# Hash attention, then a gated feed-forward block, on one core: hash bits made on four column quarters and sent by way of DRAM, a third buffer for the attention output, and another start

## The chip, the cores and the metric

The kernel runs on one core of one Trainium2 chip. The metric is the device time in microseconds, from start to end of one execution. The kernel before takes 933.71 us, the median of three executions (931.88 to 935.03).

A core has a matrix engine (TensorE, written PE in the views), a vector engine (VectorE, DVE), an activation engine (ScalarE, ACT), a general engine (GpSimd, POOL) and a queue engine (SyncE, SP). Each works through its own instructions in order, and they wait for each other by semaphores. Matrix products are written to PSUM, banks of accumulators that ScalarE and VectorE read. Transfers are issued by SyncE, ScalarE or GpSimd and run on 16 shared DMA engines.

## What is computed

Two stages. The first is attention for 4 batches x 8 heads, sequence 768, head size 64. Every query and key gets a bucket of six sign bits; a score counts only where the buckets of query and key are equal. The second is a feed-forward block over the 3072 tokens.

```python
q_bits = (np.einsum('bhsd,dk->bhsk', q, proj) > 0).astype(np.int64)   # proj: 64 x 6
k_bits = (np.einsum('bhsd,dk->bhsk', k, proj) > 0).astype(np.int64)
q_bucket = np.sum(q_bits * powers, axis=-1)
k_bucket = np.sum(k_bits * powers, axis=-1)
mask = q_bucket[:, :, :, None] == k_bucket[:, :, None, :]
scores = scale * np.matmul(q, k.transpose(0, 1, 3, 2))
scores = np.where(mask, scores, -1000000000.0)
scores = scores - np.max(scores, axis=-1, keepdims=True)
attn = np.exp(scores)
attn = attn / (np.sum(attn, axis=-1, keepdims=True) + 1e-09)
# (B,H,S,D) -> x: (B*S, H*D) = 3072 x 512
h = x @ w_in                                     # 512 x 2048
sp = np.maximum(h, 0.0) + np.log1p(np.exp(-np.abs(h)))
out = (h * erf(sp)) @ w_out                      # 2048 x 512
```

## The kernel before, where the change touches it

Heads are worked on in 16 pairs. A pair's q and k lie one head above the other, 64 partitions each. Names: `P` is 128 partitions, `S` = 768, `HS` = 384 (half a sequence), `D` = 64, `NBIT` = 6, `GC` = 3. A pair has four score groups n (two query halves, two key halves) of three score tiles c; `h` counts halves of pairs.

At the start, seven constant products in bfloat16 run on TensorE while the first loads come in:

```python
    nc.vector.memset(w_sum[:, 0, 0, 0:HS], 1.0)
    warm = w_sum[:, 0, 0, 0:HS].bitcast(BF16)
    proj_in = const.tile([P, 2 * NBIT], F32, name="proj_in")
    nc.scalar.dma_start(out=proj_in, in_=proj2)
# ... cut ...
            for n in range(WARM):                # WARM = 7
                nc.tensor.matmul(
                    out=bank("warm"),
                    lhsT=warm[:, 0:P],
                    rhs=warm[:, P : P + 512],
                    start=True,
                    stop=True,
                )
            for half in range(2):
                hash_bits(pairs[0], big, (half,))
                take_bits(pairs[0], bitp, (half,))
```

The hash bits: one float32 product per half and per q or k, each 64 output rows (32 for each head of the pair), in a PSUM tile called `bits`. ScalarE takes the sign into `qb`; VectorE writes the keys' signs, times a weight of 2**100 or 0, into `kb` for each head, and doubles the queries' signs:

```python
    def hash_bits(d, big, halves=(0, 1)):
        if halves[0] == 0:
            d["bits"] = big("bits")
        for half in halves:
            for n, what in enumerate("qk"):
                nc.tensor.matmul(
                    out=d["bits"][n * D : n * D + D, half, 0:HS],
                    lhsT=proj_sb,
                    rhs=d[what][:, half * HS : (half + 1) * HS],
                    start=True,
                    stop=True,
                )

    def sign_bits(d, bitp, cols):
        if cols.start == 0:
            for what in ("qb", "kb"):
                d[what] = bitp.tile([P, S], BF16, name=what, tag=what)
        nc.scalar.activation(
            out=d["qb"][:, cols].rearrange("p (h s) -> p h s", s=HS),
            in_=d["bits"][:, cols.start // HS : cols.stop // HS, 0:HS],
            func=AF.Sign,
            scale=2.0**100,
            bias=sgn[:, 0:1],
        )

    def spread_bits(d, cols, ab):
        nc.vector.tensor_scalar(
            out=d["kb"][ab * D : ab * D + D, cols],
            in0=d["qb"][D:P, cols],
            scalar1=weight[D:P, ab : ab + 1],
            scalar2=None,
            op0=ALU.mult,
        )

    def double_bits(d, cols):
        nc.vector.tensor_copy(out=d["qb"][D:P, cols], in_=d["qb"][0:D, cols])
```

A score tile is first the bfloat16 product of these masks (zero where the buckets agree, hugely negative elsewhere) and on top of it the float32 product of q and k:

```python
            def score(n, c):
                i, half, g = n // 4, n // 2 % 2, n % 2
                d = pairs[i]
                cols = slice(half * HS, (half + 1) * HS)
                keys = slice((g * GC + c) * P, (g * GC + c + 1) * P)
                st = d["st", n, c] = big("st")
                for part, src in enumerate(("b", "")):
                    for ab in range(2):
                        rows = slice(ab * D, ab * D + D)
                        nc.tensor.matmul(
                            out=st[:, ab, 0:HS],
                            lhsT=d["k" + src][rows, keys],
                            rhs=d["q" + src][rows, cols],
                            start=(part == 0),
                            stop=(part == 1),
                        )
```

The tiles `st` and `bits` share three slots in PSUM (`big`). ScalarE takes the exponential of a tile to SBUF (`exponential`), VectorE sums over the keys (`sum_keys`), TensorE multiplies by v (`weigh`, tile `av`) and spreads the sum (`divisor`, tile `z_ps`: four products of 32 output rows and 192 columns). ScalarE copies `av` to `x` (`leave`) and `z_ps` to `z`. The divisor goes to DRAM and back to lie on 128 partitions (`spread`, `gather`), is inverted, and comes back spread over the partitions as `r` (`widen`); `normalise` multiplies x by it and `send` stores x in `xs`. The buffers of x come from a ring of two, those of z and r together from another ring of two:

```python
            tc.tile_pool(name="xst", bufs=2) as xst,
# ... cut ...
            def home(i, what):
                if i < NPAIR - 1:
                    return xst.tile([P, S], F32, name=what, tag="x" if what == "x" else "z")
                rows = blocks[1][:, :, :].rearrange("p k t -> p (k t)")
                return rows[:, S : 2 * S] if what == "x" else rows[:, 0:S]

            def leave(h):
                i, half = divmod(h, 2)
                d = pairs[i]
                cols = slice(half * HS, (half + 1) * HS)
                if half == 0:
                    d["x"] = home(i, "x")
                nc.scalar.copy(out=d["x"][:, cols], in_=d["av"][:, 0:HS])
```

The products of TensorE stand in a fixed order, the other engines' instructions are put in order beforehand by a list scheduler in the kernel with estimated durations (`op(...)`). Bits of the next pair come at the first half of the pair before it:

```python
            chain = []
            order = [("score", 0)]
            for h in range(NH):
                order += [("score", n) for n in (2 * h + 1, 2 * h + 2) if n < NS]
                if h % 2 == 0 and h // 2 + 1 < NPAIR:
                    order.append(("bits", h // 2 + 1))
                if h >= 1:
                    order.append(("divisor", h - 1))
                order += [("weigh", 2 * h), ("weigh", 2 * h + 1)]
```

While attention runs, the weights of the second stage are fetched by GpSimd's queue in 30 pieces and converted from 64-bit words to float32 by ScalarE and VectorE.

## Time and profile before

| | before |
|---|---|
| median of three executions, us | 933.71 (931.88 to 935.03) |
| span of the profiled execution, us | 932.9 |
| TensorE busy, us | 916.8 (98%) |
| VectorE busy, us | 829.7 (89%) |
| ScalarE busy, us | 771.0 (83%) |
| GpSimd busy, us | 17.4 (2%) |
| moved by DMA | 80.92 MB, mean 87 GB/s |

The profile is of one execution. A row of a timeline reads: start in us from the start of the span, duration of the row in us, engine, line of the kernel, operation, tile written <- tiles read, shapes, how many instructions the row merges (x), and in brackets how long the engine stood idle before it and what ended that wait. A float32 product shows as two matmul records. The end of a matmul is modelled, so the distance of starts tells more than its duration. A row of the wait table reads: engine, tile and line that waited <- what ended the wait: us in total, times, longest us. Attention's lines are L358 (bits), L529 (scores), L635 (divisor), L602 (weighing), L543 (exponential), L659 (leave), L590 (sums over keys); the second stage's are L1098 and L1238.

### The profile page before, as it was taken

Reading aid. Unit: us, or ns where it says so; the run is one execution under the profiler, and the core shown is the slowest. Engines: PE = TensorE matmul, PEld = TensorE weight load, DVE = VectorE, ACT = ScalarE, POOL = GpSimd, SP = SyncE. Lnnn points to the kernel's source line nnn. Section 1 sums busy time; section 2 is a strip of 40 time slices with the busy share of each in tenths; the row PEclk is TensorE's granted clock in tenths of the full one; section 3 lists DMA queues with packets and bytes.
Section 4 is the critical chain, followed back from the end, with each engine's and each line's share of the span. In section 5 each row is a group of like instructions: output and inputs, shape, how many; then the busy total and the mean of one; then the engine's idle time right before and its main releaser. Section 6 shows DMA issues by size and latency. Waiting matters only on the chain.

```text
span 932.9 us, 12993 instructions
## 1 busy us (share of the span) xinstructions
PE 916.8 (98%) x5003; PEld 661.9 (71%) x5003; DVE 829.7 (89%) x1041; ACT 771.0 (83%) x1002; POOL 17.4 (2%) x35
## 2 busy tenths in 40 slices
PE   8999999999999999999999999999999999999996
PEld 3444444444444458888888888888888888888885
DVE  4999998999888997899999889998899789988995
ACT  5888787768876838999998998899989997899891
POOL 0000000000000000000000000000000000000000
PEclk9999999999999999999999999999999999999998
DMA  8365455576654322010212012210221111001211
GB/s 198 99 158 147 132 148 139 147 200 165 147 149 131 97 103 97 1 46 34 80 68 79 34 46 69 80 34 34 79 78 36 34 65 49 34 34 46 68 35 48
DMA packets 61398, 80.92 MB, mean 87 GB/s; under 512 B 33296, under 2 KB 46224, under 8 KB 61328
## 3 DMA queue, kind: packets, MB, share of 16 engines
q1 hardware_dynamic: 56672, 64.08, 23.9%
q0 software_dynamic: 4352, 15.73, 5.6%
q8 instruction: 41, 0.67, 0.3%
q10 hardware_dynamic: 304, 0.20, 0.1%
q14 instruction: 29, 0.24, 0.1%
HBM read 64.07 MB, written 15.93 MB: 86 GB/s over the span
## 4 chain that ended last, share of the span: by engine, by line
PE 85%; DVE 7%; DMA 4%; ACT 2%; issue 1%; SPq 0%; DVEq 0%; ACTq 0%
PE M L1238 30%; PE X L1098 27%; PE st L529 11%; PE av L602 9%; PE M L1098 3%; PE bits L358 2%; DMA xs<-x 1%; ACT e_all L543 1%; DVE x_sum L590 1%; PE z_ps L635 1%; DVE x L590 1%; DMA zd<-z 1%; DMA zc<-zd 1%; DVE x L721 1%; DMA r<-rd 1%
## 5 line engine op out<-in xcount | busy, mean ns | idle before, releaser
L1165 DVE SCALAR_TENSOR_TENSOR e<-w,e 128x1024 f32<-128x1024 f32 x144 | 173.4, 1221 | 5.8 <-ACT w L1161 3.0
L1161 ACT ACTIVATE w<-w,cq 128x1024 f32<-128x1024 f32 x144 | 160.7, 1143 | 1.9
L543 ACT ACTIVATE e_all<-st 128x768 f32<-128x768 f32 x192 | 149.1, 819 | 11.3 <-PE st L529 11.3
L529 PE MATMUL st<-q,k 64*128 64x384 f32 x768 | 156.6, 486 | 0.0
L1238 PE MATMUL M<-w_out_sb,h 128*128 128x256 f32 x576 | 140.2, 380 | 0.4 <-DVE h L1180 0.4
L602 PE MATMUL av<-e_all,v 128*64 128x385 f32 (+1 forms) x768 | 131.1, 490 | 0.0
L1098 PE MATMUL X<-x,w_in_sb 128*128 128x256 f32 x512 | 121.2, 380 | 0.0
L1238 PEld LDWEIGHTS M<-w_out_sb,h 128*128 128x128 f32 x576 | 109.3, 190 | 15.9 <-DVE h L1180 1.1
L1098 PEld LDWEIGHTS X<-x,w_in_sb 128*128 128x128 f32 x512 | 97.1, 190 | 13.8 <-ACT h L1116 0.6
L602 PEld LDWEIGHTS av<-e_all,v 128*64 128x64 f32 x768 | 52.4, 136 | 67.2 <-issue 65.4
L1238 PE MATMUL M<-wt,S 128*128 128x256 f32 x384 | 93.4, 379 | 0.4 <-DVE S L1195 0.4
L529 PEld LDWEIGHTS st<-q,k 64*128 64x128 f32 x768 | 69.1, 190 | 32.8 <-issue 32.1
L1098 PE MATMUL X<-x_sum,w_sum 128*128 128x256 f32 x344 | 81.7, 380 | 1.8 <-ACT h L1116 1.8
L1238 PEld LDWEIGHTS M<-wt,S 128*128 128x128 f32 x384 | 72.9, 190 | 10.7 <-DVE S L1195 0.8
L1098 PEld LDWEIGHTS X<-x_sum,w_sum 128*128 128x128 f32 x344 | 65.1, 190 | 12.0 <-ACT h L1116 3.3
L1116 ACT COPY h<-X 128x512 f32<-128x512 f32 x85 | 49.0, 577 | 22.3 <-PE X L1098 21.4
L1142 DVE SCALAR_TENSOR_TENSOR w<-w,e 128x1024 f32<-128x1024 f32 x48 | 58.4, 1221 | 9.6 <-ACT w L1137 9.3
L529 PE MATMUL st<-qb,kb 64*128 64x384 bf16 x384 | 63.7, 327 | 3.3 <-ACT e_all L543 3.2
L1180 DVE TENSOR_TENSOR h<-h,e 128x1024 f32<-128x1024 f32 x48 | 58.0, 1221 | 6.1 <-ACT e L1176 5.9
L659 ACT COPY x<-av 128x384 f32<-128x384 f32 x32 | 15.3, 478 | 57.4 <-DMA xs<-x 28.8
L1156 ACT ACTIVATE w<-e 128x1024 f32<-128x1024 f32 x48 | 50.4, 1050 | 13.3 <-DVE e L1152 13.0
L1152 DVE TENSOR_TENSOR e<-e,w 128x1024 f32<-128x1024 f32 x48 | 57.5, 1219 | 2.7 <-ACT e L1148 2.6
(117 smaller groups left out, 1421.0 us busy)
## 6 DMA issues: line engine op xcount, KB each, us to landing
wt<-wt SPq DMA_DIRECT2D x24, 768.0 KB, 4.3
raw<-in_w_out_dram POOLq DMA_DIRECT2D x16, 512.0 KB, 3.9
raw<-in_w_in_dram POOLq DMA_DIRECT2D x14, 512.0 KB, 4.2
v<-in_v_dram SPq DMA_DIRECT2D x32, 192.0 KB, 4.5
xs<-x SPq DMA_DIRECT2D x16, 384.0 KB, 2.4
q<-in_qkT_dram SPq DMA_DIRECT2D x30, 192.0 KB, 3.4
k<-in_qkT_dram SPq DMA_DIRECT2D x30, 192.0 KB, 4.2
r<-rd SPq DMA_DIRECT2D x30, 192.0 KB, 3.5
```

The source lines that it names most:

```text
L529: nc.tensor.matmul(out=st[:, ab, 0:HS], lhsT=d["k" + src][rows, keys], rhs=d["q" + src][rows, cols], start=(part == 0), stop=(part == 1),)
L543: nc.scalar.activation(out=e[:, :, 0:HS], in_=st[:, :, 0:HS], func=AF.Exp, scale=scale)
L602: nc.tensor.matmul(out=d["av"][rows, 0:w], lhsT=d["v"][:, g * GC + c, rows], rhs=e[:, ab, 0:w], start=(g == 0 and c == 0), stop=(g == 1 an ...
L1098: nc.tensor.matmul(out=d[where][:, u, :], lhsT=a[:, kc, f : f + P], rhs=b[:, kc, :], start=(first and u == 0 and kc == 0), stop=(last and ...
L1116: nc.scalar.copy(out=quarter(p, q), in_=st[p][where])
L1142: nc.vector.scalar_tensor_tensor(out=w, in0=w, scalar=-1.0, in1=st[p]["e", v], op0=ALU.add, op1=ALU.subtract)
L1152: nc.vector.tensor_tensor(out=s, in0=s, in1=st[p].pop(("w", v)), op=ALU.subtract)
L1156: nc.scalar.activation(out=z, in_=st[p]["s", v], func=AF.Square)
L1161: nc.scalar.activation(out=q, in_=z, func=AF.Square, bias=cq[:, j : j + 1])
L1165: nc.vector.scalar_tensor_tensor(out=s, in0=st[p].pop(("q", v, j)), scalar=ERF_Q[j][1], in1=s, op0=ALU.add, op1=ALU.mult,)
L1180: nc.vector.tensor_tensor(out=h, in0=h, in1=st[p].pop(("s", v)), op=ALU.mult)
L1238: nc.tensor.matmul(out=banks[name][:, sub, :], lhsT=a[:, u, sub * P : (sub + 1) * P], rhs=b[:, u, :], start=(c == 0 and k == 0), stop=(c = ...
```

## The change

Five things change.

- The bits of all pairs but the first come from four products of 32 output rows (16 for each head) into the four quarters of the 128 output rows: q and k, first and second half of the columns. ScalarE's sign and VectorE's weighting then work on 384 columns for all four at once.
- The signs are no longer spread by VectorE. GpSimd stores them to DRAM (`leave_bits`) and loads them back to where the masks need them (`place_bits`), into two fixed buffers whose other rows were cleared once. The bits of a pair are therefore made a half earlier in the order.
- The buffers of x become a ring of three, those of r a ring of two, and z has one of half the width. Room comes from single mask buffers and from the last sums, which use other tiles.
- The constant products at the start are five in float32 on 256 columns in place of seven in bfloat16 on 512; the small input `proj2` is loaded by GpSimd's queue, and the order of the first loads of q and k changes.
- Each half of the first pair's bits has its own PSUM tile. The first two score tiles get their q-k product first and the mask product on top of it, so that the former can run while the masks are made.

The aim is less work for TensorE, ScalarE and VectorE in the bits, no wait of ScalarE for the store of x, and an earlier full clock of TensorE.

```diff
@@ -228,9 +228,12 @@
 # ... cut ...
     QR = 32
-    WARM = 7
+    QB = QR // 2
+    WARM = 5
     proj_sb = const.tile([P, 2 * QR], F32, name="proj_sb")
     weight = const.tile([P, 2], F32, name="weight")
+    proj_q = const.tile([P, QR], F32, name="proj_q")
+    weight_q = const.tile([P, 1], F32, name="weight_q")
     ones = const.tile([P, D], F32, name="ones")
@@ -243,9 +246,9 @@
 # ... cut ...
     nc.vector.memset(w_sum[:, 0, 0, 0:HS], 1.0)
-    warm = w_sum[:, 0, 0, 0:HS].bitcast(BF16)
+    warm = w_sum[:, 0, 0, 0:HS]
     proj_in = const.tile([P, 2 * NBIT], F32, name="proj_in")
-    nc.scalar.dma_start(out=proj_in, in_=proj2)
+    nc.gpsimd.dma_start(out=proj_in, in_=proj2)
     nc.vector.memset(proj_sb, 0.0)
@@ -334,15 +350,15 @@
 # ... cut ...
         b, j = divmod(i, JP)
-        for half in range(2 if quick else 1):
-            cols = slice(half * HS, half * HS + HS) if quick else slice(0, S)
-            for n, what in enumerate("qk"):
-                queue = nc.scalar if quick and what == "k" and half == 0 else nc.sync
-                for ab in range(2):
-                    queue.dma_start(
-                        out=d[what][ab * D : ab * D + D, cols],
-                        in_=qkT[2 * i + ab, n * D : n * D + D, cols],
-                    )
+        parts = ((0, "q"), (0, "k"), (1, "k"), (1, "q")) if quick else ((None, "q"), (None, "k"))
+        for half, what in parts:
+            cols = slice(0, S) if half is None else slice(half * HS, half * HS + HS)
+            queue = nc.scalar if quick and what == "k" and half == 0 else nc.sync
+            for ab in range(2):
+                queue.dma_start(
+                    out=d[what][ab * D : ab * D + D, cols],
+                    in_=qkT[2 * i + ab, "qk".index(what) * D : "qk".index(what) * D + D, cols],
+                )
         for ab in range(2):
@@ -351,8 +367,7 @@
 # ... cut ...
     def hash_bits(d, big, halves=(0, 1)):
-        if halves[0] == 0:
-            d["bits"] = big("bits")
+        d["bits"] = big("bits")
         for half in halves:
@@ -402,10 +417,9 @@
 # ... cut ...
             tc.tile_pool(name="load", bufs=3) as load,
-            tc.tile_pool(name="bitp", bufs=2) as bitp,
+            tc.tile_pool(name="bitp", bufs=1) as bitp,
             tc.tile_pool(name="ep", bufs=1) as ep,
-            tc.tile_pool(name="sums", bufs=2) as sums,
-            tc.tile_pool(name="xst", bufs=2) as xst,
+            tc.tile_pool(name="xst", bufs=1) as xst,
             tc.tile_pool(name="rawp", bufs=2) as rawp,
@@ -414,6 +428,9 @@
 # ... cut ...
+            sg = bitp.tile([P, HS], BF16, name="sg")
+            both = [bitp.tile([P, 2, S], BF16, name=f"both{n}") for n in range(2)]
+            nc.gpsimd.memset(both[1], 0.0)
             junk = ep.tile([P, HS], BF16, name="junk")
@@ -516,14 +533,18 @@
 # ... cut ...
-            def score(n, c):
+            def score(n, c, parts=((0, "b"), (1, ""))):
 # ... cut ...
                 keys = slice((g * GC + c) * P, (g * GC + c + 1) * P)
-                st = d["st", n, c] = big("st")
-                for part, src in enumerate(("b", "")):
+                if ("st", n, c) in d:
+                    parts = ((1, "b"),)
+                else:
+                    d["st", n, c] = big("st")
+                st = d["st", n, c]
+                for part, src in parts:
                     for ab in range(2):
@@ -533,6 +554,10 @@
 # ... cut ...
                         )
 # ... cut ...
+            def plain(n, c):
 # ... cut ...
+                score(n, c, ((0, ""),))
@@ -610,9 +639,11 @@
 # ... cut ...
                 if i < NPAIR - 1:
-                    return xst.tile([P, S], F32, name=what, tag="x" if what == "x" else "z")
+                    shape, bufs = {"x": (S, 3), "z": (HS, 1), "r": (S, 2)}[what]
+                    return xst.tile([P, shape], F32, name=what, tag=what, bufs=bufs)
                 rows = blocks[1][:, :, :].rearrange("p k t -> p (k t)")
-                return rows[:, S : 2 * S] if what == "x" else rows[:, 0:S]
+                c = {"x": S, "z": 2 * S, "r": 0}[what]
+                return rows[:, c : c + (HS if what == "z" else S)]
@@ -771,23 +802,70 @@
 # ... cut ...
             def bits_of(i):
-                hash_bits(pairs[i], big)
 # ... cut ...
+                d = pairs[i]
+                d["bits"] = big("bits")
+                for n, what in enumerate("qk"):
+                    for half in range(2):
+                        row = (2 * n + half) * QR
+                        nc.tensor.matmul(
+                            out=d["bits"][row : row + QR, 0, 0:HS],
+                            lhsT=proj_q,
+                            rhs=d[what][:, half * HS : (half + 1) * HS],
+                            start=True,
+                            stop=True,
+                        )
             def sign_of(i):
-                sign_bits(pairs[i], bitp, slice(0, S))
 # ... cut ...
-            def weigh_bits(i, ab):
-                spread_bits(pairs[i], slice(0, S), ab)
 # ... cut ...
-            def copy_bits(i):
-                double_bits(pairs[i], slice(0, S))
+                nc.scalar.activation(
+                    out=sg,
+                    in_=pairs[i].pop("bits")[:, 0, 0:HS],
+                    func=AF.Sign,
+                    scale=2.0**100,
+                    bias=sgn[:, 0:1],
+                )
 # ... cut ...
+            def weigh_bits(i):
 # ... cut ...
+                nc.vector.tensor_scalar(
+                    out=sg[D:P, :],
+                    in0=sg[D:P, :],
+                    scalar1=weight_q[D:P, 0:1],
+                    scalar2=None,
+                    op0=ALU.mult,
+                )
 # ... cut ...
+            def leave_bits(i):
+                bd = pairs[i]["bd"] = dram.tile([4, 2, QB, HS], BF16, name="bd", tag="bd")
+                nc.gpsimd.dma_start(out=bd.rearrange("n a r c -> (n a r) c"), in_=sg)
 # ... cut ...
+            def place_bits(i):
 # ... cut ...
+                d = pairs[i]
+                bd = d.pop("bd")
+                for n, what in enumerate(("qb", "kb")):
+                    d[what] = both[i % 2][:, n, :]
+                for ab in range(2):
+                    nc.gpsimd.dma_start(
+                        out=both[i % 2][ab * D : ab * D + NBIT + 1, :, :].rearrange(
+                            "r w (h c) -> r (w h) c", h=2
+                        ),
+                        in_=bd[:, ab, 0 : NBIT + 1, :].rearrange("n r c -> r n c"),
+                    )
 # ... cut ...
+            def clean():
 # ... cut ...
+                nc.gpsimd.memset(both[0], 0.0)
 # ... cut ...
                 order += [("score", n) for n in (2 * h + 1, 2 * h + 2) if n < NS]
-                if h % 2 == 0 and h // 2 + 1 < NPAIR:
-                    order.append(("bits", h // 2 + 1))
+                if h == 0:
+                    order.insert(3, ("bits", 1))
+                if h % 2 and (h + 3) // 2 < NPAIR:
+                    order.append(("bits", (h + 3) // 2))
                 if h >= 1:
@@ -795,13 +873,16 @@
 # ... cut ...
                     i = n // 4
-                    after = tuple(("weigh_bits", i, ab) for ab in range(2)) + (("copy_bits", i),)
+                    after = (("place_bits", i),)
+                    if n == 0:
+                        for c in range(2):
+                            pe(plain, (n, c), 0.66)
                     for c in range(GC):
                         free = (slots[-3],) if len(slots) >= 3 else ()
-                        pe(score, (n, c), 0.82, after + free)
+                        pe(score, (n, c), 0.82 if n or c == 2 else 0.17, after + free)
                         slots.append(("exponential", n, c))
                 elif what == "bits":
-                    pe(bits_of, (n,), 1.34, (("start_pair", n), slots[-3]))
+                    pe(bits_of, (n,), 0.92, (("start_pair", n), slots[-3]))
                     slots.append(("sign_of", n))
@@ -844,7 +927,7 @@
 # ... cut ...
                     (0, 2 * h, -1),
-                    (("divisor", h), ("send", i - 1) if i == NPAIR - 1 else ("widen", i - 1)),
+                    (("divisor", h), ("spread", i - 1)),
                 )
@@ -864,16 +947,17 @@
 # ... cut ...
                     )
-                    op(sign_of, (i,), "ACT", 0.88, (0, n - 2, 9), (("bits_of", i), ("score", n - 5, 2)))
-                    for ab in (1, 0):
-                        op(weigh_bits, (i, ab), "DVE", 0.43, (0, n - 2, 1), (("sign_of", i),))
+                    op(sign_of, (i,), "ACT", 0.6, (0, n - 6, 9), (("bits_of", i), ("leave_bits", i - 1)))
+                    op(weigh_bits, (i,), "DVE", 0.33, (0, n - 6, 1), (("sign_of", i),))
+                    op(leave_bits, (i,), "POOL", 0.7, (0, n - 6, 2), (("weigh_bits", i),), late=2.6)
                     op(
-                        copy_bits,
+                        place_bits,
                         (i,),
-                        "DVE",
-                        0.35,
-                        (0, n - 2, 2),
-                        (("weigh_bits", i, 0), ("weigh_bits", i, 1)),
+                        "POOL",
+                        1.2,
+                        (0, n - 6, 3),
+                        (("leave_bits", i), ("score", n - 5, 2)) + (("clean",),) * (i == 2),
+                        late=2.6,
                     )
```

(Cut from the diff: the helper constants for the new row weights, the room for the last sums, and unchanged renamings of arguments.)

## The prediction

> **What bounds the kernel now.** I read the page first: TensorE is busy for 98% of the span, VectorE 89%, ScalarE 83%, GpSimd 2%.
>
> ```profile
> PE 916.8 (98%) x5003; PEld 661.9 (71%) x5003; DVE 829.7 (89%) x1041; ACT 771.0 (83%) x1002; POOL 17.4 (2%) x35
> PE 85%; DVE 7%; DMA 4%; ACT 2%; issue 1%; SPq 0%; DVEq 0%; ACTq 0%
> ```
>
> "Busy" is modelled for matmuls, so I looked at the starts of the matmuls in the timeline. The attention stage runs from 5.78 us (first hash-bit product) to 339.38 us (first product of the second stage); the feed-forward stage takes the other 593.5 us and the change does not touch it. Here is one stretch of attention on TensorE.
>
> ```profile
> 284.42 0.54 PE L358 MATMUL bits<-q,proj_sb 128*64 128x384 f32 x1
> 284.42 0.54 PE L358 MATMUL bits<-k,proj_sb 128*64 128x384 f32 x1
> 284.79 0.49 PE L358 MATMUL bits<-q,proj_sb 128*64 128x384 f32 x1
> ...
> 285.86 0.53 PE L635 MATMUL z_ps<-x,ones 128*32 128x192 f32 x8
> 286.32 4.10 PE L602 MATMUL av<-e_all,v 128*64 128x385 f32 x24
> 290.36 0.34 PE L529 MATMUL st<-qb,kb 64*128 64x384 bf16 x2
> 290.53 0.81 PE L529 MATMUL st<-q,k 64*128 64x384 f32 x4
> 291.17 0.33 PE L529 MATMUL st<-qb,kb 64*128 64x384 bf16 x2
> ...
> 294.94 0.34 PE L529 MATMUL st<-qb,kb 64*128 64x384 bf16 x2 [1.99 <-ACT e_all L543]
> ```
>
> The reader should see that each block starts where the one before stops: bits 1.44 us (284.42 to 285.86), divisor 0.46, weighing 4.04, then one score every 0.81. TensorE itself is the bound, so TensorE time that is removed comes off the end. And there is one hole, 1.99 us at 292.9. Two other views explain it: ScalarE's timeline, and the wait table.
>
> ```profile
> 293.69 0.48 ACT L659 COPY x<-av 128x384 f32<-128x384 f32 x1 [5.99 <-DMA xs<-x]
> ACT x L659 <- DMA xs<-x: 28.8, 7, 6.0
> ```
>
> ScalarE stood for 6 us before it could copy the result x out of PSUM, because both x buffers were still waiting to be stored; the exponentials behind it were held, the three score banks filled up, and TensorE stopped. Seven such waits, 28.8 us of ScalarE. Going through the starts of all blocks of six scores, a full block takes 4.95 us, and five of them (at 146, 167, 187, 208 and 290 us) took 5.44, 5.16, 5.03, 6.23 and 7.11: 4.2 us of TensorE lost in all.
>
> Then the start.
>
> ```profile
> 1.40 4.45 PE L749 MATMUL warm<-w_sum 128*128 128x512 bf16 x7 [1.40 <-DVE w_sum L245]
> 8.03 0.90 PE L358 MATMUL bits<-q,proj_sb 128*64 128x384 f32 x1 [0.71 <-ACT qb L371]
> 9.59 0.50 PE L529 MATMUL st<-qb,kb 64*128 64x384 bf16 x2
> 11.16 0.53 PE L529 MATMUL st<-qb,kb 64*128 64x384 bf16 x2
> 12.76 0.53 PE L529 MATMUL st<-qb,kb 64*128 64x384 bf16 x2
> 13.81 0.32 PE L529 MATMUL st<-qb,kb 64*128 64x384 bf16 x2
> ```
>
> The first scores are 1.6 us apart and only from about 13.1 us on 0.81: until then TensorE runs at half speed, although the constant products began at 1.40.
>
> **What the Trainium skill says.** "TensorE: Matmul & The Clock Gate", Part 3: a small-M product whose outputs are laid on partitions 32j lands in one of four column groups, and such products run concurrently. The trace agrees: the divisor's eight records (two per float32 product, four groups, 192 columns) go through in 0.46 us in all. "TensorEngine Tiling (Array Packing)", Key Properties: changing the tiling mode drains the array. The trace agrees: bits followed by weighing in the same 128*64 shape took 1.34 us (the first, at 18.75), followed by the 128*32 divisor 1.44. Same first page, Part 1: full clock comes after a busy free-running window of about 3.4 us. The trace fits only if the seven bfloat16 products do not count as busy: their starts lie 0.63 us apart with weight loads between, and the full clock came 3.5 us after the dense stretch began at 9.59. "SBUF — State Buffer", SBUF: two separate sides: a DMA issued by GpSimd can be held while VectorE runs a two-port operation. The trace shows issues of 0.53 us and four of 0.76, so here this costs tenths.
>
> **The change, part by part.**
>
> 1. Hash bits in four column groups. Before, q and k go in two groups, two column halves, two passes: four steps of 0.325 us (284.79 to 285.11) plus a mode change, 1.44. After, all four run at once: two steps, 0.65, and the divisor behind them has the same 128*32 shape, so the change between the two disappears: about 0.69. That is 0.75 saved at 14 pairs and 0.55 at the first (weighing follows it): 11.0 us. The scheduler's own cost in the diff says 0.92 for the new form; if it was meant for the whole, the saving falls to some 7.5. I take 10.3.
>
> 2. ScalarE and VectorE: the sign goes from 0.90 us on 768 columns to 0.58 on 384 (that form is in the trace), 15 times, 4.8 us; VectorE gives up two times 0.42 and one 0.35 for one of 0.33, 15 times, 13 us. Neither is the bound; VectorE was busy 296 of 321 us in attention, so this only keeps it from becoming the bound when the stage shortens. Worth 0 directly.
>
> 3. In place of VectorE's spreading: one store of 96 KB to DRAM and two small loads for each pair, on GpSimd's queue. From the trace, a GpSimd issue costs 0.53 to 0.67 and the one small DMA of that queue landed 2.9 us after its start. So leave 2.9, two loads 0.6 + 2.9, and with sign 0.6, weight 0.33 and queueing of 1 to 4 us on ScalarE and VectorE, a pair's bits are ready 9 to 13 us after the product. From the third pair on the order gives the chain time: bits after the scores of half h, first use after z 0.46, weighing 4.03, six scores 4.95, z 0.46, weighing 4.03, three scores 2.43, that is 16.4. Hidden, but not by much: I put 0.5 us for stray stalls. The second pair has less: its bits come after the ninth score and are needed after one weighing and three scores, 6.5 us later. There the chain of 8 to 10 us shows, while the first loads still keep the DMA engines full (the third pair's k landed at 20.8): a stall of 1 to 4 us, I take 2.0.
>
> 4. Third x buffer: leaves of pair i wait for the store of pair i-3 instead of i-2. The five stalls should go: 4.2, less something for those with a second cause, 3.7.
>
> 5. The start. Float32 warm-up products do not leave gaps, so the clock should open between 5 and 8 us instead of 13; the second half's bits get a bank of their own and no longer wait for the sign (0.71); the two plain scores fill the time in which the masks are made. Bits of the first half at 5.7, of the second when the data is there (about 7.1), nine scores at 0.81 from 7.8: the second pair's bits at about 15.1 instead of 18.75. With a late clock it is 16. I take 3.3.
>
> Sum: 10.3 + 3.7 + 3.3 - 2.0 - 0.5 = 14.8. 933.7 - 14.8 = 918.9 us.
>
> **Rivals.** (a) The round trip by DRAM is late for every pair, and the wait for the mask takes the place of the saved products. For it: a store in the old kernel took up to 5.9 us to land beside the loads, GpSimd works in order and its weight fetches wait for the exponentials, DMA is at half load. Against: 16.4 us of room. At 0.5 us a pair, 14 pairs, the time is 926; at 1 us the whole gain is gone, 933; at 2 us it is 947. (b) VectorE takes over: it was busy 296.3 of the 320.6 us from the first pair's scores to the end of attention, 92.4%. For it: the shorter stage. Against: it gives up 13 us of its own, and (296.3 - 13) / 0.924 is 307 us, where I expect TensorE to need some 310 from there on. So it is close but not the bound; were it to cost a third of the gain, the time would be 924. (c) Everything lands: full saving of 11.0, all stalls gone, 3.6 at the start and no stall at the second pair: 18.8, 914.9, just over 2%. (d) The clock does not open earlier: the start gives 1, and the time is 921.
>
> **Range and chances.** The large terms are products on the bound engine with durations read from the trace; the doubtful ones are the size of a four-group product (2.5 us), the second pair's stall (2) and rival (a). 80%: 912 to 926. Faster by over 2% needs under 915.0, nearly everything of (c): 0.22. Slower by 2% means over 952.4, rival (a) at 2.4 us in every pair: 0.03.
>
> **What would show it.** In the changed profile: bits to divisor some 0.7 us apart; blocks of six scores at 4.95 without exception, no wait of the copy L659 for the store; scores at 0.81 before 10 us; a hole before the second pair's first score, near 22 us, ended by the load of its bits; first feed-forward product near 324 and 593 us from there to the end. I am wrong if score blocks wait for the bits' load in later pairs, if the bits stay over 1 us, or if the feed-forward stage changes length.

## The result and the profile after

The changed kernel takes 920.62 us (median of four executions, 919.97 to 923.97); the kernel before took 933.61 us beside it. The ratio is 0.9869, with a 95% interval of 0.9839 to 0.9898: 13.0 us saved. The prediction was 918.9, with a range of 912 to 926.

First the page of the changed kernel: busy time by engine, then the shares of the chain that ended last.

```profile
PE 905.2 (98%) x5006; PEld 659.0 (72%) x5006; DVE 819.4 (89%) x1020; ACT 768.2 (84%) x1002; POOL 46.6 (5%) x83
PE 94%; DVE 2%; DMA 1%; SPq 1%; ACT 1%; issue 0%; POOL 0%; DVEq 0%; ACTq 0%; POOLq 0%
```

The chain is the work followed back from the last instruction, at each step to what released it. TensorE's share of it rises from 85% to 94%, VectorE's falls from 7% to 2%, while the busy shares hardly moved. By itself this does not tell what brought the time: `e1` below has the same 94% and 2%, and gains nothing that can be measured.

Now TensorE's timeline of the changed kernel, where it answers to the stretch shown of before, and the first product of the feed-forward stage.

```profile
284.44 0.52 PE L812 MATMUL bits<-q,proj_q 128*32 128x384 f32 x2
284.45 0.52 PE L812 MATMUL bits<-k,proj_q 128*32 128x384 f32 x2
...
285.11 0.51 PE L666 MATMUL z_ps<-x_sum,ones 128*32 128x192 f32 x8
285.55 4.09 PE L631 MATMUL av<-e_all,v 128*64 128x384 f32 x24
289.57 0.34 PE L550 MATMUL st<-both 64*128 64x384 bf16 x2
...
325.56 1.78 PE L1183 MATMUL M<-x,w_in_sb 128*128 128x256 f32 x7 [0.57 <-ACT x L690]
```

From bits to divisor are now 0.67 us (284.44 to 285.11), where they were 1.44. Attention ends at 325.56 instead of 339.38, 13.8 us earlier. From there to the end are 593.7 us (919.3 - 325.6), against 593.5 before. So the whole difference lies in attention, and the starts of matmuls account for it:

| where TensorE gained or lost | predicted, us | measured, us | how it is read |
|---|---|---|---|
| bits | +10.3 | +11.6 | 14 x (1.44 + 0.46 - 0.67 - 0.44) = 11.0, and 1.34 - 0.78 at the first |
| long score blocks | +3.7 | +4.2 | all five are gone |
| the start | +3.3 | +0.4 | second pair's bits at 18.34 instead of 18.75 |
| second pair's masks | -2.0 | -1.6 | score block from 23.16 takes 6.59 instead of 4.95 |
| stray holes | -0.5 | -0.8 | one, at 66 us |
| sum | 14.8 | 13.8 | |

The table says where on TensorE the time went, not yet which part of the change brought it. The line with the large miss is the start.

```profile
1.40 6.34 PE L780 MATMUL warm<-w_sum 128*128 128x256 f32 x10 [1.40 <-DVE w_sum L248]
7.66 0.90 PE L373 MATMUL bits<-q,proj_sb 128*64 128x384 f32 x1
...
10.42 1.87 PE L550 MATMUL st<-q,k 64*128 64x384 f32 x8
...
18.34 0.52 PE L812 MATMUL bits<-q,proj_q 128*32 128x384 f32 x2
...
26.71 0.32 PE L550 MATMUL st<-both 64*128 64x384 bf16 x1 [0.96 <-ACT e_all L568]
27.23 0.33 PE L550 MATMUL st<-both 64*128 64x384 bf16 x1 [0.20 <-DMA both<-bd]
...
67.08 0.34 PE L550 MATMUL st<-both 64*128 64x384 bf16 x2 [0.63 <-ACT e_all L568]
```

The constant products lasted until 7.66 instead of 5.78, so the first bits came 1.9 us later than before. Weight loads of the changed kernel tell why:

```profile
2.67 0.50 PEld L780 LDWEIGHTS warm<-w_sum 128*128 128x128 f32 x2 [0.77 <-PE warm L780]
3.95 0.50 PEld L780 LDWEIGHTS warm<-w_sum 128*128 128x128 f32 x2 [0.78 <-PE warm L780]
```

Each product waits for the one before it: every product asks for a new tile of a pool that has one buffer. They are 1.28 us apart, two passes of 0.64 each.

The other two holes belong to the way by DRAM. Here is GpSimd's timeline of the changed kernel (rows of issues), then ScalarE's at the hole of 66 us.

```profile
20.77 0.55 POOL L841 DMA_DIRECT2D bd<-sg  x1 [16.92 <-DVE sg L831]
24.51 1.14 POOL L850 DMA_DIRECT2D both<-bd  x2 [3.19 <-DMA bd<-sg]
...
52.65 0.55 POOL L841 DMA_DIRECT2D bd<-sg  x1 [7.95 <-DVE sg L831]
57.70 1.15 POOL L850 DMA_DIRECT2D both<-bd  x2 [4.50 <-PE st L550]
58.84 1.14 POOL L456 DMA_DIRECT2D raw<-in_w_in_dram  x2
```

```profile
64.52 0.68 ACT L470 ACTIVATE keep<-raw 128x512 f32<-128x512 f32 x1 [4.01 <-DMA raw<-in_w_in_dram]
```

The second pair's bits are stored at 20.77, loaded from 24.51, and the last load lands at 27.18, where the mask product of 27.23 waits for it. The 0.8 us at 66 come indirectly: ScalarE stands 4 us for a piece of the feed-forward weights, which GpSimd issued only behind the mask loads of that pair. That this order is the cause is argued from these rows; a run meant to show it did not settle it (below).

### The profile page after: what moved, and what is told of

The parts are those of the page before. It is cut to its first block, busy times and chain, and to the rows that moved or that the text cites. A ratio compares the mean times of both kernels' runs of the same rounds, so it can differ in the third digit from the quotient of the medians.

```text
span 919.3 us, 13120 instructions
## 1 busy us (share of the span) xinstructions
PE 905.2 (98%) x5006; PEld 659.0 (72%) x5006; DVE 819.4 (89%) x1020; ACT 768.2 (84%) x1002; POOL 46.6 (5%) x83
## 4 chain that ended last, share of the span: by engine, by line
PE 94%; DVE 2%; DMA 1%; SPq 1%; ACT 1%; issue 0%; POOL 0%; DVEq 0%; ACTq 0%; POOLq 0%
PE M L1323 31%; PE X L1183 28%; PE st L550 16%; PE av L631 14%; PE M L1183 3%; PE z_ps L666 1%; PE bits L812 1%; DMA q<-in_qkT_dram 1%; SPq L358 1%; DVE e L1237 0%; DMA bd<-sg 0%; DVE h L1265 0%; SPq L363 0%; DMA both<-bd 0%; DVE S L1280 0%
## 5 line engine op out<-in xcount | busy, mean ns | idle before, releaser
L568 ACT ACTIVATE e_all<-st 128x768 f32<-128x768 f32 x192 | 151.2, 813 | 14.6 <-PE st L550 12.4
L1183 PEld LDWEIGHTS X<-x,w_in_sb 128*128 128x128 f32 x512 | 97.0, 190 | 13.8 <-ACT h L1201 0.6
L550 PE MATMUL st<-both 64*128 64x384 bf16 x384 | 63.1, 324 | 1.8 <-ACT e_all L568 1.6
L1205 DVE TENSOR_TENSOR h<-X,h 128x512 f32<-128x512 f32 x65 | 44.8, 689 | 16.4 <-PE X L1183 15.4
```

The source lines that it names most:

```text
L550: nc.tensor.matmul(out=st[:, ab, 0:HS], lhsT=d["k" + src][rows, keys], rhs=d["q" + src][rows, cols], start=(part == 0), stop=(part == 1),)
L568: nc.scalar.activation(out=e[:, :, 0:HS], in_=st[:, :, 0:HS], func=AF.Exp, scale=scale)
L1183: nc.tensor.matmul(out=d[where][:, u, :], lhsT=a[:, kc, f : f + P], rhs=b[:, kc, :], start=(first and u == 0 and kc == 0), stop=(last and ...
```

## The experiments

"Attention ends" is the first feed-forward product in the profile. The theory after the table was that the removed products bring 11.6 and the third x buffer 4.2, and that VectorE's lighter load is worth nothing by itself. The rival was that VectorE had bound attention together with TensorE, and that its relief is a part of both lines. The kernel before was timed again beside each group of runs and took 931.65 to 933.61 us there. Each ratio is to the executions beside it, so between groups the ratios compare and the times only roughly.

### Without the four groups

The changed kernel with bits in two groups, as in the kernel before, and everything else (DRAM, buffers, start) as changed.

```diff
-                d["bits"] = big("bits")
-                for n, what in enumerate("qk"):
-                    for half in range(2):
-                        row = (2 * n + half) * QR
-                        nc.tensor.matmul(out=d["bits"][row : row + QR, 0, 0:HS], lhsT=proj_q, ...)
+                hash_bits(pairs[i], big)
# sg is P x S, the sign is taken on 768 columns; bd and the loads follow that layout
```

> The changed kernel with the bits' products put back to the old form (two column groups, 64 rows each, both halves in turn, sign on 768 columns), still sent by way of DRAM. Theory (TensorE is the bound, the four-group form is worth its TensorE time): bits 1.44 us instead of 0.67 and divisor 0.46 instead of 0.44, so 15 pairs cost 11.6 us more, some 932 us. Rival (the gain comes from VectorE and ScalarE, freed by the new route): near 921. If the larger store (192 KB a pair) comes late, more than 933.

Measured: 930.77 us (20 executions, 929.63 to 932.57), ratio 0.9996 (0.9986 to 1.0005). TensorE's timeline of this kernel:

```profile
273.97 0.54 PE L372 MATMUL bits<-q,proj_sb 128*64 128x384 f32 x1
...
275.41 0.53 PE L665 MATMUL z_ps<-x_sum,ones 128*32 128x192 f32 x8
```

The 1.44 us are back (273.97 to 275.41), attention ends at 336.21, 10.6 later than in the changed kernel. Without the four groups the rest of the change gains nothing that this many executions can tell. Its one block of scores that is long is the second pair's. `e1` also gives ScalarE its old sign on 768 columns back (0.91 us in place of 0.59), but that is not where the time went. In the 200 us from 100 on, TensorE's busy time, the first figure after the length, is 200.00: its own products fill the stage.

```profile
100.00:300.00 200.00, 200.00 (x1420) 91.22 (x1414) 182.25 (x241) 158.17 (x287) 27.87 (x50) 1.00 0.59 165
```

### VectorE's load put back

The changed kernel, and for every pair some VectorE work whose result nothing uses: `e9` one multiplication of 0.42 us and one copy of 0.35 us, which brings VectorE's work for the bits to 15 x (0.32 + 0.42 + 0.35) = 16.4 us, just under the 15 x (2 x 0.42 + 0.35) = 17.9 of before. `e8` has two multiplications (22.7 us); `e7` is `e8` with two x buffers.

```diff
+            def burden(i, k):
+                if k < 2:
+                    nc.vector.tensor_scalar(
+                        out=spare[0:D, :], in0=both[i % 2][D:P, 1, :], scalar1=ones[D:P, 0:1],
+                        scalar2=None, op0=ALU.mult,
+                    )
+                else:
+                    nc.vector.tensor_copy(out=spare[D:P, :], in_=spare[0:D, :])
# for every pair, after weigh_bits: k in (1, 2) in e9, k in range(3) in e7 and e8
```

> The changed kernel with two buffers of x and with VectorE work of the old size put back (for each pair two operations of 0.42 us and one of 0.35 that write to a spare tile). Theory (VectorE's relief took the waits for the store away): waits of the copy of x return, 20 us or more on ScalarE, TensorE loses 3 to 5 us, some 924 us. Rival (the order of the instructions, above all loads before store in SyncE's queue, took them away): as with two buffers alone, some 921.

> The changed kernel with the same VectorE work put back and its three buffers of x kept. Theory (third buffer and relief each suffice for most of it): no waits for the store, within 1 us of the changed kernel. Rival (VectorE is close to being the bound): TensorE loses some of the 13 us, 924 or more.

> The changed kernel, three buffers of x, with one operation of 0.43 us and one of 0.35 put back on VectorE for each pair, so that with the new weighing its work on the bits is what it was before (some 17 us in all; the two runs before had put back 19 us on top of 5). Theory (VectorE was a bound beside TensorE, and needs its relief for TensorE's saving to show): attention ends 5 us or more later than in the changed kernel, time 926 to 929 us. Rival (VectorE only turns into the bound when given more than it ever had): within 1.5 us of the changed kernel, 922 at most.

Measured: `e9` 926.07 us (925.36 to 927.67), ratio 0.9939 (0.9920 to 0.9958); `e8` 933.31, ratio 1.0017 (1.0006 to 1.0027); `e7` 932.75, ratio 1.0001 (0.9989 to 1.0012). The burdens of `e7` and `e8` are larger than what the change took away, so the fair one is `e9`: its ratio is 0.9939 against 0.9869, and attention ends at 331.51, 5.9 us later than in the changed kernel, though TensorE's instructions are the same. The chain that ended last now has 22% of VectorE, where the changed kernel has 2%. Below it stand rows of `e9`'s wait table for TensorE, then one of these waits on TensorE's timeline:

```profile
PE 63%; DVE 22%; DMA 4%; issue 3%; ACT 1%; SPq 0%; POOL 0%; DVEq 0%; POOLq 0%; ACTq 0%
```

```profile
PE av L632 <- DVE ev L697: 4.0, 6, 1.4
PE st L551 <- DMA both<-bd: 1.4, 2, 0.8
```

```profile
209.01 0.51 PE L667 MATMUL z_ps<-x_sum,ones 128*32 128x192 f32 x8
210.91 1.83 PE L632 MATMUL av<-e_all,v 128*64 128x384 f32 x10 [1.40 <-DVE ev L697]
```

From divisor to weighing TensorE needs 0.44 us; here it takes 1.90, because VectorE has not yet read its column (`ev`) of the weighing before out of PSUM. The same 200 us of attention in each kernel, from the tables by stretch (columns: us, then busy time of PE, PEld, DVE, ACT and POOL, clock, DMA share, GB/s), of before, after, and `e9`:

```profile
100.00:300.00 200.00, 196.73 (x1392) 90.58 (x1390) 183.89 (x253) 152.75 (x277) 10.04 (x19) 1.00 0.58 153
```

```profile
100.00:300.00 200.00, 200.00 (x1473) 92.87 (x1470) 188.31 (x252) 160.63 (x294) 28.37 (x50) 1.00 0.62 166
```

```profile
100.00:300.00 200.00, 195.66 (x1438) 91.41 (x1436) 189.79 (x264) 156.72 (x290) 29.75 (x51) 1.00 0.61 160
```

Where the 5.9 us lie in `e9`: all steps from divisor to weighing add up to 18.4 us, to 14.0 in the changed kernel, and its long score blocks to 3.8 against 2.4. Two of these, of 6.21 us from 202.13 and 5.99 from 244.25 instead of 4.95, hold the two waits for masks of the table above. So VectorE's load also makes the way by DRAM late.

In the changed kernel TensorE is never idle in these 200 us and VectorE is at 94%. With VectorE's old load TensorE stands for 4.3 us of them while VectorE is only 1.5 us busier, at 95%. With 6.3 us more load (`e8`, `e7`) it comes to 190.6 and 191.1 us; no run has it above 96% in this stretch. The kernel's scheduler orders the instructions anew for each variant, so `e9` shows what the load costs together with the order that follows from it.

### The x buffers alone

`e2` is the changed kernel with two x buffers; `e4` is the kernel before with the new rings (three x, two r, one z of half width, the old sums' room used for them) and nothing else.

```diff
# e2
-                    shape, bufs = {"x": (S, 3), "z": (HS, 1), "r": (S, 2)}[what]
+                    shape, bufs = {"x": (S, 2), "z": (HS, 1), "r": (S, 2)}[what]
# e4, on the kernel before
-            tc.tile_pool(name="sums", bufs=2) as sums,
-            tc.tile_pool(name="xst", bufs=2) as xst,
+            tc.tile_pool(name="xst", bufs=1) as xst,
# ... cut ...
-                    return xst.tile([P, S], F32, name=what, tag="x" if what == "x" else "z")
+                    shape, bufs = {"x": (S, 3), "z": (HS, 1), "r": (S, 2)}[what]
+                    return xst.tile([P, shape], F32, name=what, tag=what, bufs=bufs)
```

> The changed kernel with two buffers of x instead of three, nothing else. Theory: the copy of x out of PSUM waits for the store of two pairs before and TensorE loses again what it lost before, 4.2 us in score blocks longer than 4.95 us: some 925 us. Rival (the waits went because VectorE has less to do and normalises earlier): no such blocks, 920.6.

> The kernel before with the new buffers alone (three of x, two of r, a half-width z, last sums in other tiles). Theory: the five long score blocks go, 4.2 us, to 929.5 us. Rival (the waits need VectorE's relief): 933.5.

Measured: `e2` 921.28 us, ratio 0.9875 (0.9850 to 0.9900), attention ends at 326.05, only 0.5 later than with three. `e4` 932.28, ratio 0.9992 (0.9981 to 1.0004), attention ends at 338.97. ScalarE's row of the wait table for `e2`, then for `e4` and a row of TensorE's timeline there:

```profile
ACT x L690 <- DMA xs<-x: 11.6, 3, 4.5
```

```profile
ACT z L653 <- DMA zd<-z: 5.7, 7, 2.3
```

```profile
271.95 0.70 PE L528 MATMUL st<-qb,kb 64*128 64x384 bf16 x2 [0.60 <-DVE kb L382]
```

With three buffers but the loaded VectorE (`e4`) the wait for the store is gone, and others stand in its place: for the single z buffer, and for VectorE spreading the masks. The long blocks add up to 3.65 us there, against 4.2 before. In `e1`, which has three buffers too but no spreading by VectorE, only the second pair's is left. In `e2` the wait for the store is down from 28.8 us in seven to 11.6 in three. Two score blocks behind such waits, 5.31 us from 102.81 and 5.98 from 239.88, cost 1.4 us; that attention ends only 0.5 later is because the start, the second pair and the hole near 66 us happened to cost 0.9 less.

The shorter wait for the store does not need VectorE's lighter load. `e7` has two x buffers and more load on VectorE than the kernel before, and its row is:

```profile
ACT x L691 <- DMA xs<-x: 12.0, 7, 3.4
```

So what the third buffer adds to the rest of the change is some 1.4 us by these runs, and nothing with VectorE loaded (below). Most of the five stalls that the prediction gave to the store went with the rest, but which part of it shortened that wait stays open: the buffers of r and z and the order of the instructions changed as well, and no run separates them.

All kernels with these three things varied:

| kernel | bits in groups | VectorE's work for bits, us | x buffers | attention ends, us | time, us | ratio |
|---|---|---|---|---|---|---|
| before | 2 | 17.9 | 2 | 339.4 | 933.61 | 1 |
| `e4` | 2 | 17.9 | 3 | 339.0 | 932.28 | 0.9992 |
| `e1` | 2 | 6.3 | 3 | 336.2 | 930.77 | 0.9996 |
| `e8` | 4 | 22.7 | 3 | 338.4 | 933.31 | 1.0017 |
| `e7` | 4 | 22.7 | 2 | 337.5 | 932.75 | 1.0001 |
| `e9` | 4 | 16.4 | 3 | 331.5 | 926.07 | 0.9939 |
| `e2` | 4 | 4.8 | 2 | 326.1 | 921.28 | 0.9875 |
| after | 4 | 4.8 | 3 | 325.6 | 920.62 | 0.9869 |

From after to `e9` VectorE gets 11.6 us more and the end moves by 5.9, half of it. From `e9` to `e8` it gets 6.3 more and the end moves by 6.9, but a part of that is TensorE's clock. Here is the end of attention in `e8`, and the row of its table by stretch, in which the third figure from the end is the granted clock:

```profile
331.11 6.74 PE L632 MATMUL av<-e_all,v 128*64 128x384 f32 x24 [3.50 <-DVE ev L697]
338.43 1.78 PE L1195 MATMUL M<-x,w_in_sb 128*128 128x256 f32 x7 [0.58 <-ACT x L691]
```

```profile
331.00:335.00 4.00, 3.90 (x12) 1.48 (x14) 3.72 (x8) 0.00 (x0) 0.00 (x0) 0.50 0.02 2
```

TensorE has stood 3.5 us for VectorE, the clock is at half, and from the last weighing to the end are 7.32 us, which are 4.67 in `e9`. Without these 2.65 us `e8` ends at 335.8. In `e7` the same step takes 6.36 us, and without the 1.7 too many it ends at 335.8 as well. So 6.3 us of load cost 4.3, and with this load a third x buffer makes no difference. With two groups, taking 11.6 away (`e4` to `e1`; the start and the second pair's masks differ there too) moves the end by only 2.8 and does not lower the ratio, because TensorE's own products then hold it. The two savings need each other: beside the rest of the change, the four groups without the relief come to 0.9939, the relief without the groups to 0.9996, both to 0.9869.

### The start, and the second pair

The theory was that the start failed because of the spacing of the float32 products. The rival was that an early start is worth nothing, because the second pair's masks come by DRAM. `e3` is the changed kernel with the old constant products; `e5` makes the second pair's masks as before, in two groups and by VectorE, without DRAM; `e6` is both. `e5` and `e6` leave out clearing the second mask buffer before the fourth pair, so rows of the second head's masks of later odd pairs still hold the second pair's bits. `e10` is `e6` with that clearing (one more step on GpSimd in place of the one at the start). `e11` has float32 products, all into one tile.

```diff
# e3 (and e6, e10)
-    WARM = 5
+    WARM = 7
-    warm = w_sum[:, 0, 0, 0:HS]
+    warm = w_sum[:, 0, 0, 0:HS].bitcast(BF16)
-    nc.gpsimd.dma_start(out=proj_in, in_=proj2)
+    nc.scalar.dma_start(out=proj_in, in_=proj2)
-                    out=bank("warm")[:, 0 : 2 * P],
+                    out=bank("warm"),
-                    rhs=warm[:, P:HS],
+                    rhs=warm[:, P : P + 512],
# e5 (and e6, e10, e11)
+                if i == 1:
+                    hash_bits(d, big)
+                    return
# and near_sign, near_spread, near_double (sign_bits, spread_bits, double_bits into both[1])
# in place of sign_of, weigh_bits, leave_bits, place_bits for i == 1
# e10 and e11
-            nc.gpsimd.memset(both[1], 0.0)
+            op(clean_other, (), "POOL", 1.4, (0, 4), (("score", 7, 2),), late=0.3)   # before place_bits(3)
# e11
+            warm_bank = bank("warm")
-                    out=bank("warm")[:, 0 : 2 * P],
+                    out=warm_bank[:, 0 : 2 * P],
```

> The changed kernel with the old constant products (seven in bfloat16 on 512 columns) and the small input on ScalarE's queue. Theory: the new float32 constant products cost 1.9 us more of the start than the old ones (6.27 against 4.38 us) and bring no earlier full clock, so the old ones are quicker: second pair's bits at some 16.5 to 17.5 us instead of 18.34, time some 1 us shorter, 919.5. Rival (the float32 ones are what brings the full clock at 11 us instead of 13): second pair's bits at 18.5 or later, 921 or more.

> The changed kernel, with the bits of the second pair alone made the old way (two column groups, spread by VectorE, no DRAM); its start unchanged. Theory (the second pair's masks come at about 27 us because their way through DRAM queues behind the first loads): the 1.64 us hole before the second pair's first score goes, the old product costs 0.55 more there: 1.1 us less, first feed-forward product at 324.5 us instead of 325.6. Rival (the hole is a wait for a score bank or for the loads of q and k): it stays.

> As the one before, with the old constant products and the old queue of the small input too. Theory: now nothing swallows the quicker start (second pair's bits at 15.5 us) and the 6.6 us hole is gone: first feed-forward product near 321.5 us, some 4 us less than the changed kernel, 916.5 us. Rival (the loads, saturated until 20 us, bound the first two pairs in any case): the hole moves to another wait and the time stays at 920.

> The changed kernel with the second pair's bits by VectorE, the old constant products and the old queue of the small input; its mask buffer is cleared before the fourth pair. Theory: as with the uncleared one, first feed-forward product at 321.9 us, 916.5 us, clearly under the changed kernel. Rival: the clearing (1.4 us of GpSimd) delays the fourth pair's masks and shows as a new hole.

> As e10, but with the changed kernel's float32 constant products, all into one tile so that none waits for the one before. Theory (they were slow for that wait alone, 0.63 us a pass instead of 0.43): they end near 5.7 us, the clock opens at 8 us or before, second pair's bits at 15.3 us, first feed-forward product at 321.4 us or as e10. Rival (weight loads, not the wait, keep them apart): they end at 7.7 us as in the changed kernel, and the first feed-forward product comes at 324 us.

| kernel | constant products | second pair's masks | its bits at, us | attention ends, us | time, us | ratio (95%) |
|---|---|---|---|---|---|---|
| after | float32, spaced | DRAM | 18.34 | 325.6 | 920.62 | 0.9869 (0.9839 to 0.9898) |
| `e3` | bfloat16 | DRAM | 15.47 | 327.6 | 921.66 | 0.9885 (0.9864 to 0.9907) |
| `e5` | float32, spaced | VectorE | 17.54 | 323.9 | 918.81 | 0.9852 (0.9834 to 0.9870) |
| `e6` | bfloat16 | VectorE | 15.83 | 321.9 | 916.74 | 0.9833 (0.9813 to 0.9854) |
| `e10` | bfloat16 | VectorE | 16.37 | 321.7 | 916.36 | 0.9838 (0.9820 to 0.9856) |
| `e11` | float32, dense | VectorE | 15.71 | 322.0 | 916.68 | 0.9841 (0.9821 to 0.9860) |

`e3` has the early start that the prediction wanted, and gains nothing. TensorE's timeline, then GpSimd's, of `e3`:

```profile
5.78 0.90 PE L373 MATMUL bits<-q,proj_sb 128*64 128x384 f32 x1
...
7.11 0.50 PE L373 MATMUL bits<-q,proj_sb 128*64 128x384 f32 x1
...
15.47 0.52 PE L812 MATMUL bits<-q,proj_q 128*32 128x384 f32 x2
...
22.07 0.81 PE L550 MATMUL st<-q,k 64*128 64x384 f32 x4
26.75 0.32 PE L550 MATMUL st<-both 64*128 64x384 bf16 x1 [3.87 <-DMA both<-bd]
27.69 0.50 PE L550 MATMUL st<-both 64*128 64x384 bf16 x1 [0.62 <-DMA both<-bd]
```

```profile
17.91 0.55 POOL L841 DMA_DIRECT2D bd<-sg  x1 [14.61 <-DVE sg L831]
23.60 1.14 POOL L850 DMA_DIRECT2D both<-bd  x2 [5.14 <-DMA bd<-sg]
```

The bits come 2.9 us earlier than in the changed kernel, their store is issued 2.9 earlier, and the loads 0.9 earlier: the store landed after 5.0 us instead of 3.1, beside the first loads. The masks arrive at 26.6 and 27.6 us, no earlier than in the changed kernel (26.6 and 27.2), and TensorE stands until then. The whole early start is swallowed by that hole, and the clock falls behind it:

```profile
28.00:31.00 3.00, 3.00 (x13) 1.93 (x12) 0.00 (x0) 0.81 (x1) 0.00 (x0) 0.50 0.46 154
```

Between 27 and 32 us the mean clock is 0.66, that is about 3.4 us at half, which by this reckoning cost some 1.7. With the last mask landing 0.5 later this is why attention ends 2.0 us later than in the changed kernel. With the masks made by VectorE (`e5`) the hole is gone; then, and only then, is the early start worth something: 323.9 to 321.9 from `e5` to `e6`. The full clock came at another time in each of these profiles, so the starts scatter: in the changed kernel and its variants the second pair's bits came between 17.25 and 18.65 us with the spaced products (seven runs), between 15.47 and 16.80 with bfloat16 or dense ones (five). The two microseconds between the groups are more than that scatter; the 0.4 of the first table, between two single executions, are not. TensorE's timeline of `e10`:

```profile
7.11 0.85 PE L373 MATMUL bits<-q,proj_sb 128*64 128x384 f32 x1
...
16.37 0.54 PE L373 MATMUL bits<-q,proj_sb 128*64 128x384 f32 x1
...
17.71 4.05 PE L630 MATMUL av<-e_all,v 128*64 128x385 f32 x24
21.69 0.34 PE L549 MATMUL st<-both 64*128 64x384 bf16 x2
```

The score block after 21.69 takes 4.95 us and no block of six scores in this execution is longer. `e10` leaves nothing out and takes 916.36 us (916.06 to 916.56). Its ratio is 0.9838 against 0.9869 of the changed kernel, with intervals that overlap slightly, and attention ends 3.9 us earlier. `e6`, `e11` and `e12` lie within 0.4 us of it.

`e11` shows that float32 was not at fault. TensorE's timeline:

```profile
1.39 4.63 PE L780 MATMUL warm<-w_sum 128*128 128x256 f32 x10 [1.39 <-DVE w_sum L248]
5.96 0.90 PE L373 MATMUL bits<-q,proj_sb 128*64 128x384 f32 x1
```

The same ten passes end at 5.96 instead of 7.66 when they share a tile and need not wait for each other: (5.96 - 1.39)/10 is 0.46 us a pass. After that `e11` is as good as `e10`.

### The weight piece behind the masks

`e12` is `e10` with the weight piece whose lateness stood before the hole of 66 us issued by SyncE.

```diff
-                queue = nc.sync if n < 2 else nc.gpsimd
+                queue = nc.sync if n < 2 or n == 5 else nc.gpsimd
```

> As e10, with the sixth piece of weights fetched by SyncE's queue. Theory (the hole of 0.8 us near 65 us is that piece, held on GpSimd's queue behind the load of the bits): the hole goes, first feed-forward product 0.8 us earlier than e10. Rival: the piece is late for another reason, or SyncE's loads are delayed by it: no gain.

Measured: 916.39 us, ratio 0.9837 (0.9819 to 0.9855), the same as `e10`. There is no hole near 61 us, but `e10` had none either, so this tells nothing of the cause. Another hole appeared, on TensorE's timeline, and attention ends at 323.6 here:

```profile
182.15 0.53 PE L549 MATMUL st<-both 64*128 64x384 bf16 x2 [1.19 <-DMA both<-bd]
```

Those mask loads were issued from 174.72 on, right behind SyncE's store and reload of x (174.18 and 174.56), and landed at 182.10 and 182.30. Such stray holes of about a microsecond move from kernel to kernel; why each lies where it does stays open.

## Why the prediction was right, and where it was wrong

The time was right to 1.7 us (918.9 against 920.62), but two steps failed and one cause was misplaced. That it came so close is partly luck: in the first table the start brought 2.9 us less than predicted, and bits, score blocks and the second pair's masks together 2.2 more.

**Bits (step 1): right.** "About 0.69" measured 0.67; "0.75 saved at 14 pairs" was 0.77, and the divisor gave 0.02 more since no mode change stands before it. The discount to 10.3 for a slower form was not needed: 11.6. `e1` confirms it from the other side, 10.6 without the four groups.

**VectorE (step 2): wrong.** "Neither is the bound … Worth 0 directly" fails: `e9` puts the old load back, leaves TensorE's work as it is, and attention is 5.9 us longer. So of 13.8 us, 5.9 depended on the relief. It did not show as a term of its own because it was already inside the others: without it the saved products turn in part into waits, 4.4 us before weighings and 1.4 in score blocks. The Trainium skill, "Perfetto Trace Analysis", section Identifying the Most-Contended Engine, says of occupancy that for VectorE "it is also a fair measure of how close you are to roofline". Here 92% before left little room: no run came above 96% between 100 and 300 us. (The 320.6 us that the 92.4% refer to begin at the second pair's bits, not at the first pair's scores as rival (b) has it.) Rival (b) got 307 us for VectorE; that is so near TensorE's 310 that it should have been read as two engines that hold each other up, not as "not the bound".

**DRAM (step 3): right in kind and size.** Hidden for nearly every pair: -0.8 in all, 0.5 predicted; rival (a) does not hold. At the second pair -1.6, 2.0 predicted, and the trace shows the masks' load as what ended it. "DMA: Bandwidth & Descriptors" of the skill, section Anatomy of one DMA — SWDGE (gpsimd) path, gives a fixed cost of about 2 us, most of it the receipt of the write. The 15 stores of the changed kernel landed after 2.0, 3.7 and 5.0 us (least, median, most): the page's figure is the least here, and most took nearly twice that. (Of the longer issues on GpSimd's queue, the trace of before has three, of 0.76 and 0.77 us, not four.)

**Third x buffer (step 4): size right, cause not as given.** The five stalls are gone, 4.2. But "leaves of pair i wait for the store of pair i-3 instead of i-2" names a reason that alone does nothing measurable: `e4` has it, is at 0.9992 and keeps 3.65 us of long blocks; `e2` lacks it and gets 1.4 of them back. Most of the stalls went with the rest of the change, and what shortened the wait for the store stays open.

**The start (step 5): wrong, 0.4 for 3.3.** Two things failed. "Float32 warm-up products do not leave gaps" was false as they are written: each waits for its tile, and they end 1.9 us late; that was readable in the code. And the step took the second pair's earlier bits as a gain at the end, while step 3 put a stall of 2.0 behind them that ends when a load lands; `e3` shows that the earlier bits only lengthen the stall. The two terms were not independent and must not be added. Also wrong is the reading that bfloat16 products "do not count as busy". In `e3` the clock is full by 7.11 us, 1.3 us after the first dense product, which leaves no room for a busy window of 3.4 us that began there. In `e10` the same products start at the same times up to 7.11 and run at half speed for some 2 us more. "TensorE: Matmul & The Clock Gate", Part 1, says that the window runs freely and that the same kernel can warm up sooner or later; these two runs agree. Why it came only at 13.1 us in the kernel before, with a gap of 0.7 in its bits, stays open.

## What to carry to other kernels

When an engine at over 90% stands beside the bound, take work off both before judging either: here the relief of VectorE alone brought nothing measurable, the four groups without it less than half, and both together 13 us. Do not add the gain of an earlier start to a stall that a transfer ends. A trip by DRAM can free an engine at little cost in steady state (0.8 us of holes here), but the first user in the pipeline should get the short way.

## What the runs showed of the hardware that was not expected

- VectorE between 30 and 315 us waited for 11 us in all in the kernel before (the largest row 10.9 for the divisor's transfer) and for 8 in the changed one, though its busy share was 93% and 94% there. Some 10 us more of its idle time in each are short gaps between instructions that follow each other.
- The full clock of TensorE came between 7.1 us (`e3`) and about 13.1 (before) over the runs here; `e3` and `e10` have the same matmul starts up to 7.11 us and then differ.
- The granted clock fell to half after a hole of TensorE of 3.5 us or more, in `e3` (3.87 us), `e7` and `e8` (3.50 us each), and stayed there for 3.4, 3.4 and 6.8 us. No hole of up to 1.99 us did that here.
- Ten passes of a constant float32 product took 0.46 us each in one tile and 0.63 in a new tile each, at the same half clock.
